# Linear attention into a two-expert MoE: routing and dispatch on two batches at a time, and the first loads in another order

## The chip, the cores and the metric

The kernel runs on one core of one Trainium2 chip. The metric is device time in microseconds (us) of one execution. TensorE is PE in the profile (its weight loads are PEld), VectorE is DVE, ScalarE is ACT, GpSimd is POOL, SyncE is SP; SP issues most of the DMAs of the loads, POOL the stores.

## The reference, cut to what matters

```python
# q, k, v: (8, 8, 576, 64) float32; batch, head, sequence, head dim
q_s = softmax(q, axis=-1)
k_s = softmax(k, axis=2)                       # over the sequence
kv  = einsum('bhsd,bhse->bhde', k_s, v)
a   = einsum('bhsd,bhde->bhse', q_s, kv)
x   = a.transpose(0, 2, 1, 3).reshape(4608, 512)

logits = x @ w_gate + modality_bias[modality_id]     # 8 experts
e_idx  = argmax(logits, axis=1)
gate_w = softmax(logits)[row, e_idx]
for e in range(8):                                   # w1[e]: 512x1024, w2[e]: 1024x512
    out[e_idx == e] = gate_w * (relu(x @ w1[e]) @ w2[e])
```

With this draw the bias of the modality decides the expert, so that two experts, here called the left and the right one, take all rows. The kernel loads the weights of these two alone, and has a loop over all experts behind it that runs only where this does not hold.

## The kernel before, in words

The eight batches are handled in four phases of two. Each batch passes through two functions:

- `stage_a(b)`: ACT takes exp of k and of q (`ek`, `eq`), POOL casts v to bf16 (`vb`, two instructions), PE forms k'v (`kv_ps`, 36 matmuls), transposes q (`tp_ps`, copied to `et` by DVE and ACT), DVE divides kv into the block-diagonal `kvbd`; from that PE makes the gate's matrix (`g_ps`, copied to `gx`) and the logits of the batch's 576 rows (`lg_ps`, 20 matmuls). The rest of the function, the routing, is a chain of some 35 DVE instructions on five columns (a batch is five tiles of 64, 128, 128, 128, 128 rows, one column each): the logits `lw`, `lg`, the maximum, `isa` (1 for the left expert), two matmuls `r_ps` that count rows, running offsets `aoff`, five permutation matrices `perm`, and `hhi`, `hlo`, `hv`, which place row numbers by a matmul. `hv` is made by POOL.
- `stage_b(b)`, the dispatch: for each of the five tiles PE forms the attention rows (`x_ps`), DVE scales them (`x_sb`), PE transposes and permutes them (`xT_ps`, by `perm`), and the tile is written twice into `xs`, the row buffer of both experts: from the left by ACT (the register offset from `aoff_i`) and from the right by DVE. Then five matmuls `id_ps` (`hlo` by `hv`) and an addition to `lst` by DVE give the row numbers.

After each second batch `places()` turns `lst` into the store indices `idx`, and `ffn` runs the two experts on the two passes of 512 rows that are full by then: `h_ps` (32 matmuls), relu to `hT` by ACT (three of four) or DVE, `y_ps` (32 matmuls), a copy to `y_sb`, and an indirect store issued by POOL. After the last phase two passes more, of 384 rows, follow.

Engines work in order, each from its own queue. The order in the queues is made ahead of time by a list scheduler: code under `tc.high_priority` (the two stages and the loads) goes ahead of `ffn`, which fills PE between. PSUM pools are `mm` (3 buffers: kv_ps, tp_ps, kvT_ps, x_ps, xT_ps), `ff` (3: h_ps, y_ps) and `sp` (2: g_ps, lg_ps, r_ps, id_ps).

SP issues the loads in the order batch 0, batch 1, weights of the left expert, batch 2, weights of the right expert, batch 3, and so on (k, v, q, 1152 KB each; the weights in four parts of 1024 KB). All go through one rotating pool of staging buffers, `st`: a load waits until its buffer's former content was cast. The weights are cast to `W` by ACT (parts 0 and 2) and DVE (parts 1 and 3). Seven small loads (bias, gate matrix in four parts, modality in two) are issued by ACT at the start.

```python
stage = ctx.enter_context(tc.tile_pool(name="stage", bufs=5))
...
for b in range(B):
    with tc.high_priority(offset=AHEAD):
        stage_a(b)
        stage_b(b)
        if b == 0:
            load_weights(eids[0], 0, (nc.scalar, nc.vector))
            load_batch(2)
```

Of the kernel before, what the change touches and what calls it, by code (L numbers as in the profile page):

```python
# [11 lines left out]
FP32 = mybir.dt.float32  # L12
# [8 lines left out]
P = 128  # L21
# [21 lines left out]
def kernel(  # L43
# [28 lines left out]
    NPH = 4  # L72

# [9 lines left out]
    stage = ctx.enter_context(tc.tile_pool(name="stage", bufs=5))  # L83
# [25 lines left out]

    bias_b = const.tile([P, 2, E], FP32)  # L110
    nc.scalar.dma_start(
# [5 lines left out]
    for h2 in range(2):  # L117
        for hl in range(2):
            nc.scalar.dma_start(
# [114 lines left out]
    kvbd_b = [persist.tile([P, NP, P], BF16, name=f"kvbd{i}") for i in range(2)]  # L234
    gx_b = [persist.tile([P, NP, 18], BF16, name=f"gx{i}") for i in range(2)]
    et_b = [persist.tile([P, NP, 640], BF16, name=f"et{i}") for i in range(2)]
    vb_b = [persist.tile([P, NJ, 2, 130], BF16, name=f"vb{i}") for i in range(2)]
    for i in range(2):
        nc.vector.memset(kvbd_b[i], 0.0)
# [3 lines left out]
        nc.gpsimd.memset(et_b[i][:, :, 576:640], 0.0)  # L243
# [44 lines left out]
    def stage_a(b):  # L288
        i = b % 2
        kvbd, gx, et, vb = kvbd_b[i], gx_b[i], et_b[i], vb_b[i]  # L290
# [5 lines left out]
        for hp in range(2):  # L296
            nc.gpsimd.tensor_copy(  # L297
# [60 lines left out]
        for t in range(NT):  # L358
            for p_ in range(NP):
# [6 lines left out]
                )  # L366

        qi = small.tile([P, NT * H], FP32, name="qi")
        nc.vector.tensor_scalar_add(out=qi, in0=view(lg_ps, [[18, NT * NP], [1, 2]], 16), scalar1=1e-9)
        nc.vector.reciprocal(out=qi, in_=qi)  # L370
        lw = small.tile([P, NT * NP, 2, E], FP32, name="lw")
        nc.vector.tensor_tensor(
            out=lw,
            in0=view(lg_ps, [[18, NT * NP], [8, 2], [1, 8]]),
            in1=view(qi, [[2, NT * NP], [1, 2], [0, 8]]),
            op=ALU.mult,
        )
        lg = small.tile([P, NT, E], FP32, name="lg")
        nc.vector.reduce_sum(out=lg, in_=view(lw, [[H * E, NT], [1, E], [E, H]]), axis=AX.X)
# [345 lines left out]
```

## Time and profile before

| | |
|---|---|
| median of 3 runs | 285.17 us (284.83 to 285.68) |
| the profiled execution: time | 284.43 us |
| its span, first to last instruction | 282.7 us |
| PE busy | 208.1 us (74% of the span), 1657 matmuls |
| DVE busy | 174.7 us (62%), 566 instructions |
| ACT busy | 115.8 us (41%), 161 instructions |
| POOL busy | 75.3 us (27%), 86 instructions |
| HBM read, written | 36.80 MB, 9.96 MB |

In the rows, numbers are microseconds from the span's start. A row of the timeline has the start, the duration, the engine, the line, the operation with what it writes and reads, and in brackets how long the engine was idle before and what ended that. A row of a wait has the engine that waited, whom for, the total, the number and the longest. PE's ends are modelled; a row that merges matmuls ("x4") runs from the first start to the last end.

### The profile page before, as it was taken

The page shows a single profiled execution, that of the slowest core. Times are in us where ns is not written, and L with a number is a line of the kernel's source. Part 1 is how long each engine was busy: PE and PEld are TensorE (multiplying, and loading weights), DVE is VectorE, ACT ScalarE, POOL GpSimd, SP SyncE. Part 2 cuts the span into 40 slices and gives each one's busy share as a digit, 9 for nine tenths or more (in the row PEclk, how much of TensorE's full clock was granted, in tenths as well). Part 3 has the DMA queues.
Part 4 walks back from the last instruction along what each step waited for, and adds up shares of the span by engine and source line. Part 5 has one row for each costly group of instructions (what it writes and reads, how often), then busy time and mean ns, then how long its engine had stood idle before and what let it go on. Part 6 is the DMA issues. An engine that isn't in the chain of part 4 may idle for free.

```text
span 282.7 us, 4628 instructions
## 1 busy us (share of the span) xinstructions
PE 208.1 (74%) x1657; PEld 116.2 (41%) x1657; DVE 174.7 (62%) x566; ACT 115.8 (41%) x161; POOL 75.3 (27%) x86
## 2 busy tenths in 40 slices
PE   0044358236998999787897979889997799999910
PEld 0033237124644644453463445445543344455500
DVE  4595865687479858858773897688678421313310
ACT  1365354623775692195158323422622414141200
POOL 7143203013103711351360033123205223224120
PEclk9999999999999999999999899999999999999985
DMA  5999999969959996143030002101201203021020
GB/s 166 329 392 405 387 390 400 363 205 330 319 202 332 344 377 265 39 140 141 0 151 0 0 3 111 39 1 43 108 2 44 104 37 114 37 111 66 2 87 5
DMA packets 20716, 46.59 MB, mean 165 GB/s; under 512 B 3023, under 2 KB 3023, under 8 KB 20688
## 3 DMA queue, kind: packets, MB, share of 16 engines
q1 hardware_dynamic: 15872, 36.70, 36.2%
q0 software_dynamic: 3040, 9.44, 8.7%
q10 hardware_dynamic: 1776, 0.10, 0.4%
q8 instruction: 15, 0.25, 0.4%
q14 instruction: 13, 0.11, 0.1%
HBM read 36.80 MB, written 9.96 MB: 165 GB/s over the span
## 4 chain that ended last, share of the span: by engine, by line
PE 34%; issue 23%; DVE 6%; POOL 6%; ACT 4%; DMA 2%; POOLq 0%; DVEq 0%; ACTq 0%
PE y_ps L582 15%; PE h_ps L568 10%; POOL hv L452 3%; PE xT_ps L508 2%; PE kv_ps L306 2%; DVE xs L519 2%; DMA st<-in_v_dram 2%; POOL out_dram L595 2%; ACT xs L518 1%; ACT et L328 1%; PE tp_ps L318 1%; DVE x_sb L500 1%; PE x_ps L492 1%; PE id_ps L535 1%; DVE y_sb L591 1%
## 5 line engine op out<-in xcount | busy, mean ns | idle before, releaser
L568 PE MATMUL h_ps<-xs,W 128*128 128x512 bf16 (+1 forms) x320 | 76.0, 378 | 1.7 <-ACT xs L518 0.7
L582 PE MATMUL y_ps<-W,hT 128*128 128x512 bf16 x304 | 73.2, 379 | 1.7 <-DVE y_sb L591 1.1
L595 POOL DMA_INDIRECT out_dram<-y_sb,idx x38 | 37.5, 986 | 71.9 <-DVE y_sb L591 57.3
L518 ACT CAST xs<-xT_ps 128x512 f32 (+2 forms) x40 | 21.9, 546 | 71.1 <-PE xT_ps L508 67.2
L576 ACT ACTIVATE hT<-h_ps 128x512 bf16<-128x512 f32 (+1 forms) x60 | 34.0, 581 | 28.4 <-PE h_ps L568 21.8
L568 PEld LDWEIGHTS <-W 128*128 128x128 bf16 x320 | 30.3, 99 | 29.7 <-issue 4.4
L582 PEld LDWEIGHTS <-hT 128*128 128x128 bf16 x304 | 28.6, 98 | 30.8 <-issue 1.9
L452 POOL TENSOR_TENSOR hv<-hhi,vals 128x570 bf16<-128x570 bf16 x8 | 12.6, 1577 | 90.1 <-DVE hhi L448 90.1
L500 DVE TENSOR_TENSOR x_sb<-x_ps,scl 128x512 bf16<-128x512 f32 (+1 forms) x40 | 27.3, 683 | 7.6 <-PE x_ps L492 7.5
L508 PE MATMUL xT_ps<-perm,x_sb 128*128 128x128 bf16 (+1 forms) x160 | 19.0, 234 | 14.6 <-DVE x_sb L500 14.6
L519 DVE CAST xs<-xT_ps 128x512 f32 (+2 forms) x40 | 25.4, 634 | 5.8 <-ACT xs L518 5.2
L306 PE MATMUL kv_ps<-vb,ek 64*128 64x129 bf16 x288 | 18.3, 251 | 14.0 <-POOL vb L297 14.0
L591 DVE COPY y_sb<-y_ps 128x512 f32<-128x512 f32 x30 | 20.3, 685 | 12.7 <-PE y_ps L582 11.6
L578 DVE TENSOR_SCALAR hT<-h_ps 128x512 bf16<-128x512 f32 (+1 forms) x20 | 13.2, 660 | 22.4 <-PE h_ps L568 22.4
L297 POOL CAST vb<-st 128x1152 bf16<-128x1152 f32 x16 | 18.0, 1152 | 33.5 <-DMA st<-in_v_dram 33.5
L508 PEld LDWEIGHTS <-x_sb 128*128 128x128 bf16 (+1 forms) x160 | 11.0, 104 | 27.3 <-DVE x_sb L500 22.6
L306 PEld LDWEIGHTS <-ek 64*128 64x128 bf16 x288 | 14.8, 110 | 15.7 <-ACT ek L294 10.9
L295 ACT ACTIVATE eq<-st 128x2304 bf16<-128x2304 f32 x8 | 17.1, 2135 | 6.5 <-DMA st<-in_q_dram 6.5
L294 ACT ACTIVATE ek<-st 128x2304 bf16<-128x2304 f32 x8 | 17.0, 2124 | 6.2 <-PE kv_ps L306 3.7
L492 PE MATMUL x_ps<-kvbd,et 128*128 128x128 bf16 (+1 forms) x160 | 18.1, 244 | 1.5 <-ACT et L328 1.5
L318 PE MATMUL tp_ps<-ident,eq 128*128 128x128 bf16 x144 | 14.4, 253 | 5.3 <-DVE et L326 2.7
L318 PEld LDWEIGHTS <-eq 128*128 128x128 bf16 x144 | 11.5, 115 | 10.8 <-issue 6.3
(123 smaller groups left out, 203.0 us busy)
## 6 DMA issues: line engine op xcount, KB each, us to landing
st<-in_k_dram SPq DMA_DIRECT2D x8, 1152.0 KB, 8.1
st<-in_v_dram SPq DMA_DIRECT2D x8, 1152.0 KB, 8.0
st<-in_q_dram SPq DMA_DIRECT2D x8, 1152.0 KB, 6.4
st<-in_moe_w_dram SPq DMA_DIRECT2D x8, 1024.0 KB, 9.9
out_dram<-y_sb,idx POOLq DMA_INDIRECT x38, 2.7
mraw<-in_moe_modality_id_dram ACTq DMA_DIRECT2D x2, 36.0 KB, 5.1
wg_f<-in_moe_w_gate_dram ACTq DMA_DIRECT2D x4, 4.0 KB, 6.8
bias_b<-n_moe_modality_bias_dram ACTq DMA_DIRECT2D x1, 8.0 KB, 5.3
```

The source lines that it names most:

```text
L306: nc.tensor.matmul(out=kv[hg][:, 130 * hp : 130 * hp + 129], lhsT=ek[rows, j, P * hp : P * hp + P], rhs=vb[rows, j, hp, 0:129], start=(j = ...
L318: nc.tensor.transpose(out=view(tp, [[2 * nj * 64, 2], [1, 64]], hp * nj * 64 + jj * 64), in_=eq[:, c0 + jj, P * hp : P * hp + P], identity ...
L452: nc.gpsimd.tensor_tensor(out=hv, in0=view(hhi, [[NSL, NT], [0, 3], [1, NSL]]), in1=view(vals, [[3, NT], [1, 3], [0, NSL]], b * NT * 3), o ...
L500: nc.vector.tensor_tensor(out=x_sb[0:T], in0=view(x_ps, [[Dh, H], [1, Dh]], 0, (0, T)), in1=view(scl, [[1, H], [0, Dh]], t * H, (0, T)), o ...
L508: nc.tensor.matmul(out=xT_ps[:, kd, 0:T], lhsT=view(x_sb, [[1, P]], kd * P, (0, T)), rhs=perm[0:T, t, 0:T], start=True, stop=True,)
L518: wa = nc.scalar.copy(out=window(a, passes_a[ph], T, ph == NPH - 1), in_=xT_ps[:, :, 0:T])
L519: wb = nc.vector.tensor_copy(out=window(a + right, passes_b[ph], T, ph == NPH - 1, True), in_=xT_ps[:, :, 0:T])
L568: nc.tensor.matmul(out=h_ps[:, 0:w], lhsT=W[:, slot, kd * F + f * P : kd * F + (f + 1) * P], rhs=xs[:, kd, lo : lo + w], start=(kd == 0), ...
L576: nc.scalar.activation(out=hT[:, f, 0:w], in_=h_ps[:, 0:w], func=ACT.Relu)
L582: nc.tensor.matmul(out=y_ps, lhsT=hT[:, kf, t * P : (t + 1) * P], rhs=W[:, slot, W2 + kf * D : W2 + (kf + 1) * D], start=(kf == 0), stop=( ...
L591: nc.vector.tensor_copy(out=y_sb, in_=y_ps)
L595: store = nc.gpsimd.indirect_dma_start(out=out, out_offset=bass.IndirectOffsetOnAxis(ap=ix[:, c : c + 1], axis=0), in_=y_sb, in_offset=Non ...
```

## The change

1. The loads of batch 0 are issued first, and the seven small loads behind them on SP's queue instead of ahead on ACT's.
2. `stage_a` ends at `lg_ps`. The routing is a function of its own, `route(pr)`, on the ten columns of two batches; the first part (`qi`, `lw`) still runs per batch. `stage_b` becomes `dispatch(pr)`: ten tiles, one accumulation of ten `id_ps` matmuls, one addition to `lst`.
3. Both copies of a tile into `xs` are made by ACT; DVE no longer loads the offsets into registers.
4. `vb` of batches 0 and 1 is cast by DVE.
5. `kvbd` and `et` have three buffers instead of two, the staging pool four instead of five, `hlo`, `hhi`, `hv`, `lw` one instead of two.
6. The loads of the weights come after `stage_a` of batches 0 and 1, ahead of routing and dispatch; `places()` and the indices come under the high priority.

The layout of the weight loads is the same in both versions (128 partitions a part).

```diff
-    stage = ctx.enter_context(tc.tile_pool(name="stage", bufs=5))
+    stage = ctx.enter_context(tc.tile_pool(name="stage", bufs=4))
...
+    load_batch(0)
     bias_b = const.tile([P, 2, E], FP32)
-    nc.scalar.dma_start(
+    nc.sync.dma_start(
         out=bias_b,
...
-    load_batch(0)
...
-            nc.gpsimd.tensor_copy(
+            (nc.vector if b < 2 else nc.gpsimd).tensor_copy(
                 out=view(vb, [[Dh, 2], [260, NJ], [1, Dh]], 130 * hp),
...
+        lgs[b] = lg_ps
+
+    def route(pr):
+        b = 2 * pr
+        qi = small.tile([P, NT2 * H], FP32, name="qi")
+        lw = small.tile([P, NT2 * NP, 2, E], FP32, name="lw", bufs=1)
+        for i in range(2):
+            lg_ps = lgs.pop(b + i)
+            qv = qi[:, i * NT * H : (i + 1) * NT * H]
+            nc.vector.tensor_scalar_add(out=qv, in0=view(lg_ps, [[18, NT * NP], [1, 2]], 16), scalar1=1e-9)
+            nc.vector.reciprocal(out=qv, in_=qv)
+            nc.vector.tensor_tensor(
+                out=lw[:, i * NT * NP : (i + 1) * NT * NP],
...
-        lg = small.tile([P, NT, E], FP32, name="lg")
-        nc.vector.reduce_sum(out=lg, in_=view(lw, [[H * E, NT], [1, E], [E, H]]), axis=AX.X)
+        lg = small.tile([P, NT2, E], FP32, name="lg")
+        nc.vector.reduce_sum(out=lg, in_=view(lw, [[H * E, NT2], [1, E], [E, H]]), axis=AX.X)
...
-        perm = sb.tile([P, NT, P], BF16, name="perm")
-        for t in range(NT):
+        perm = sb.tile([P, NT2, P], BF16, name="perm")
+        for t in range(NT2):
...
-        hlo = sb.tile([P, NT, P], BF16, name="hlo")
+        hlo = sb.tile([P, NT2, P], BF16, name="hlo", bufs=1)
...
-        hv = sb.tile([P, NT, 3, NSL], BF16, name="hv")
+        hv = sb.tile([P, NT2, 3, NSL], BF16, name="hv", bufs=1)
         nc.gpsimd.tensor_tensor(
             out=hv,
...
+    def dispatch(pr):
+        scl, perm, hlo, hv = sc.pop(pr)
+        for b in (2 * pr, 2 * pr + 1):
+            kvbd, et = kvbd_b[b % NB], et_b[b % NB]
...
+                engines=[ENG.Activation],
...
-            wb = nc.vector.tensor_copy(
-                out=window(a + right, passes_b[ph], T, ph == NPH - 1, True), in_=xT_ps[:, :, 0:T]
-            )
+                wb = nc.scalar.copy(
+                    out=window(a + right, passes_b[pr], T, pr == NPH - 1, True), in_=xT_ps[:, :, 0:T]
+                )
...
-    for b in range(B):
+    for ph in range(NPH):
         with tc.high_priority(offset=AHEAD):
-            stage_a(b)
-            stage_b(b)
-            if b == 0:
-                load_weights(eids[0], 0, (nc.scalar, nc.vector))
-                load_batch(2)
...
+            for b in (2 * ph, 2 * ph + 1):
+                stage_a(b)
+                if b < 2:
+                    load_weights(eids[b], b, (nc.scalar, nc.vector))
+                if b + 2 < B:
+                    load_batch(b + 2)
+            route(ph)
+            dispatch(ph)
             idb, ab, sel = places()
```

How the change moves instructions is seen at three places. A number behind a name is that of its buffer; the lines of the changed program stand some 20 lower than before for the same operation.

The first is DVE's queue in the dispatch ahead of the first `ffn`, from the first scaled tile of batch 1 on, before the change:

```order
L500 TENSOR_TENSOR x_sb_677<-x_ps_672,scl_630 64x512
L436 TENSOR_TENSOR slot_646<-slot_646,aoff_173 128x5
L658 TENSOR_SCALAR ok_3396<-aoff_173 1x1
L659 TENSOR_SCALAR ok_3396<-aoff_173 1x1
L438 TENSOR_SCALAR hi_650<-slot_646 128x5
L442 SCALAR_TENSOR_TENSOR lo_652<-hi_650,slot_646 128x5
L448 TENSOR_TENSOR hhi_656<-iota_row_116,hi_650 128x190
L481 TENSOR_LOAD aoff_i_175
L444 TENSOR_TENSOR hlo_654<-iota_row_116,lo_652 128x640
L519 ISA
L519 COPY xs_171<-xT_ps_679 128x4x64
L500 TENSOR_TENSOR x_sb_691<-x_ps_686,scl_630 128x512
```

The five permutation matrices stand ahead of the first scaled tile there. The same place now, from the permutation matrices of the first pair on:

```order
L449 TENSOR_SCALAR perm_519<-iota_row_116,pos_516 128x128 x10
L455 TENSOR_TENSOR slot_530<-slot_530,pos_516 128x10
L521 TENSOR_TENSOR x_sb_574<-x_ps_569,scl_509 128x512
L456 TENSOR_TENSOR slot_530<-slot_530,aoff_173 128x10
L458 TENSOR_SCALAR hi_534<-slot_530 128x10
L462 SCALAR_TENSOR_TENSOR lo_536<-hi_534,slot_530 128x10
L468 TENSOR_TENSOR hhi_540<-iota_row_116,hi_534 128x380
L464 TENSOR_TENSOR hlo_538<-iota_row_116,lo_536 128x1280
L521 TENSOR_TENSOR x_sb_588<-x_ps_583,scl_509 128x512
L562 TENSOR_TENSOR lst_204<-lst_204,id_ps_706 128x114
```

Ten matrices, and `hhi` and `hlo` of twice the width, come in one piece between the first tile and the third; the copies to `xs` are gone from this queue. PE has the ten `id_ps` matmuls after the `x_ps` of the third tile.

The second is DVE's queue at the routing that follows the first `ffn` pass, from the sum of the gate on. Before (batch 2):

```order
L400 TENSOR_REDUCE gsum_1119<-lg_1101 128x5
L429 TENSOR_SCALAR perm_1133<-iota_row_116,pos_1130 128x128
L401 TENSOR_SCALAR gsum_1119<-gsum_1119 128x5
L429 TENSOR_SCALAR perm_1133<-iota_row_116,pos_1130 128x128
L402 RECIPROCAL gsum_1119<-gsum_1119 128x5
L429 TENSOR_SCALAR perm_1133<-iota_row_116,pos_1130 128x128
L405 TENSOR_TENSOR scl_1123<-qi_1096,gsum_1119 128x20 x2
L429 TENSOR_SCALAR perm_1133<-iota_row_116,pos_1130 128x128 x2
L435 TENSOR_TENSOR slot_1139<-slot_1139,pos_1130 128x5
L500 TENSOR_TENSOR x_sb_1170<-x_ps_1165,scl_1123 64x512
L436 TENSOR_TENSOR slot_1139<-slot_1139,aoff_173 128x5
L578 TENSOR_SCALAR hT_775<-h_ps_818 128x512
```

And now (batches 2 and 3):

```order
L415 TENSOR_REDUCE gsum_1196<-lg_1178 128x10
L449 TENSOR_SCALAR perm_1210<-iota_row_116,pos_1207 128x128
L416 TENSOR_SCALAR gsum_1196<-gsum_1196 128x10
L449 TENSOR_SCALAR perm_1210<-iota_row_116,pos_1207 128x128
L417 RECIPROCAL gsum_1196<-gsum_1196 128x10
L449 TENSOR_SCALAR perm_1210<-iota_row_116,pos_1207 128x128
L420 TENSOR_TENSOR scl_1200<-qi_1170,gsum_1196 128x40 x2
L449 TENSOR_SCALAR perm_1210<-iota_row_116,pos_1207 128x128 x7
L455 TENSOR_TENSOR slot_1221<-slot_1221,pos_1207 128x10
L521 TENSOR_TENSOR x_sb_1251<-x_ps_1246,scl_1200 64x512
L456 TENSOR_TENSOR slot_1221<-slot_1221,aoff_173 128x10
L598 TENSOR_SCALAR hT_831<-h_ps_850 128x512
```

The first scaled tile, and the relu behind it, now follow ten matrices instead of five. In the two later phases the first scaled tile stands ahead of the ten, the second behind them.

The third is ACT's queue in the dispatch ahead of the first `ffn`. Before (batch 1):

```order
L518 ISA
L518 COPY xs_171<-xT_ps_679 128x4x64
L518 ISA
L518 COPY xs_171<-xT_ps_693 128x4x128
L282 CAST W_172<-st_755 128x2048
L518 ISA
L518 COPY xs_171<-xT_ps_707 128x4x128
```

And now:

```order
L538 ISA
L538 COPY xs_171<-xT_ps_643 128x4x64
L285 CAST W_172<-st_461 128x2048
L539 ISA
L539 COPY xs_171<-xT_ps_643 128x4x64
L538 ISA
L538 COPY xs_171<-xT_ps_657 128x4x128
L539 ISA
L539 COPY xs_171<-xT_ps_657 128x4x128
```

Each tile takes two copies of ACT in a row, and a cast of the weights stands between two of them.

More of the change, by code (lines that the diff above doesn't have):

```diff
@@ L415, in stage_a @@
         nc.vector.tensor_tensor_scan(
-            out=aoff[:, o + 1 : o + 1 + NT],
-            data0=ones[:, 0:NT],
+            out=aoff[:, o + 1 : o + 1 + NT2],
+            data0=ones[:, 0:NT2],
             data1=r_ps[:, 1, :],
@@ L532, in stage_b @@
         id_ps = sp_ps.tile([P, 3, NSL], FP32, name="id_ps", tag="sp")
-        for t in range(NT):
-            T = tsz[t]
+        for c in range(NT2):
+            T = tsz[c % NT]
             nc.tensor.matmul(
                 out=id_ps,
-                lhsT=hlo[0:T, t, :],
-                rhs=hv[0:T, t, :, :],
-                start=(t == 0),
-                stop=(t == NT - 1),
+                lhsT=hlo[0:T, c, :],
+                rhs=hv[0:T, c, :, :],
+                start=(c == 0),
+                stop=(c == NT2 - 1),
```

215 lines of the change are left out of this document (105 added, 110 removed).

## The prediction

> **What bounds the kernel now.** I read first the busy time by stretch, cut where the work changes, then PE's waits there, then the timeline of the stretch ahead of the first `ffn`. Columns: from:to, length, then busy time of PE, PEld, DVE, ACT, POOL, each with its instructions, PE's granted clock, DMA share, GB/s.
>
> ```profile
> 0.00:72.00 72.00, 28.90 (x295) 22.62 (x295) 48.44 (x162) 31.05 (x30) 19.05 (x34) 1.00 0.94 334
> 72.00:98.50 26.50, 24.78 (x210) 14.27 (x210) 19.80 (x68) 17.03 (x20) 8.73 (x8) 1.00 0.85 301
> 98.50:122.50 24.00, 21.15 (x186) 11.03 (x185) 18.23 (x65) 11.91 (x19) 6.68 (x7) 1.00 0.58 220
> 122.50:144.50 22.00, 18.90 (x147) 9.62 (x145) 16.43 (x55) 10.81 (x17) 6.62 (x7) 1.00 0.29 102
> 144.50:168.00 23.50, 19.52 (x176) 10.71 (x175) 15.94 (x57) 11.81 (x17) 5.50 (x5) 0.93 0.07 24
> 168.00:197.00 29.00, 26.08 (x254) 14.04 (x252) 22.42 (x75) 9.23 (x17) 7.30 (x7) 1.00 0.12 47
> 197.00:221.06 24.06, 20.21 (x162) 10.37 (x160) 18.78 (x65) 9.69 (x18) 7.78 (x8) 1.00 0.17 66
> 221.06:269.65 48.59, 48.55 (x241) 23.49 (x240) 13.61 (x24) 14.23 (x26) 12.49 (x13) 1.00 0.16 60
> 269.65:282.70 13.05, 0.00 (x0) 0.00 (x0) 1.03 (x4) 0.00 (x0) 1.19 (x2) 0.66 0.12 45
> PE id_ps L535 <- POOL hv L452: 6.0, 6, 1.4
> PE r_ps L396 <- DVE isa L392: 3.2, 5, 1.1
> PE xT_ps L508 <- DVE x_sb L500: 2.7, 4, 0.8
> PE g_ps L352 <- ACT kvT L349: 1.8, 1, 1.8
> ```
>
> Three parts. A head of 72 us, in which PE is mostly idle and the DMA is busy, until the first `ffn`. A middle of 149.1 us (72 to 221.06) in which PE works 130.6 (its six rows added) and stands for 18.4. An end of 61.6 us, pure `ffn` and the last stores, which the change leaves alone. So PE bounds all from 72 on; the time can only move with the start of the first `ffn` and with the 18.4 us. The four waits above are those of the middle: 13.7 of the 18.4. DVE, at 111.6 of 149.1 us, has room: taking work from it pays only where PE waits for it.
>
> **The head: loads.**
>
> ```profile
> SPq L100 <- DMA bias_b<-n_moe_modality_bias_dram: 4.8, 1, 4.8
> DMA to landing us min/median/max: 5.4/7.6/14.5
> 15.75 2.12 ACT L295 ACTIVATE eq<-st 128x2304 bf16<-128x2304 f32 x1 [4.95 <-DMA st<-in_q_dram]
> 18.77 2.12 ACT L294 ACTIVATE ek<-st 128x2304 bf16<-128x2304 f32 x1 [0.89 <-DMA st<-in_k_dram]
> 25.33 2.12 ACT L295 ACTIVATE eq<-st 128x2304 bf16<-128x2304 f32 x1 [1.58 <-DMA st<-in_q_dram]
> ```
>
> The second load waited 4.8 us for the bias: only so many DMAs are in flight. Now k, v and q go out together, and at 3.0 us apiece (18.77 - 15.75) q of batch 0 lands at about 12.3 instead of 15.75. But in the changed queue k of batch 1 waits for the landing of that q, behind the small loads: 12.3 plus the shortest landing, 5.4, is 17.7; v follows at 20.7, q at 23.7. So batch 1 is complete 1.6 us earlier, not 3.4. The seven small loads, behind that q, land near 13 to 14.5 by my estimate, just as DVE wants them; if later, all of batch 0 shifts with them, since DVE has the bias ahead of `kinv`.
>
> **The head: two stages, one route, ten tiles.**
>
> ```profile
> 43.73 1.94 PE L306 MATMUL kv_ps<-vb,ek 64*128 64x129 bf16 x16
> 51.12 0.68 PE L360 MATMUL lg_ps<-gx,et 128*128 128x18 bf16 x20 [0.48 <-DVE gx L356]
> 55.06 0.23 DVE L392 SCALAR_TENSOR_TENSOR isa<-kk,key,valid 128x5 bf16<-128x5 f32 x1
> 57.34 0.68 DVE L500 TENSOR_TENSOR x_sb<-x_ps,scl 64x512 bf16<-64x512 f32 x1
> 65.39 0.69 DVE L500 TENSOR_TENSOR x_sb<-x_ps,scl 128x512 bf16<-128x512 f32 x1 [0.39 <-PE x_ps L492]
> 66.13 0.61 PE L508 MATMUL xT_ps<-perm,x_sb 128*128 128x128 bf16 x4 [0.79 <-DVE x_sb L500]
> 67.21 0.69 DVE L500 TENSOR_TENSOR x_sb<-x_ps,scl 128x512 bf16<-128x512 f32 x1 [0.53 <-PE x_ps L492]
> 71.99 0.61 PE L568 MATMUL h_ps<-xs,W 128*128 128x512 bf16 x1
> L282 ACT CAST W<-st 128x2048 bf16<-128x2048 f32 x4 | 7.6, 1891 | 0.0
> L284 DVE CAST W<-st 128x2048 bf16<-128x2048 f32 x4 | 4.9, 1218 | 0.0
> L297 POOL CAST vb<-st 128x1152 bf16<-128x1152 f32 x16 | 18.0, 1152 | 33.5 <-DMA st<-in_v_dram 33.5
> L379 DVE TENSOR_REDUCE lg<-lw 128x40 f32<-128x320 f32 x8 | 5.8, 726 | 0.2
> L429 DVE TENSOR_SCALAR perm<-iota_row,pos 128x128 bf16<-128x128 bf16 x40 | 8.0, 242 | 0.0
> ```
>
> In batch 1 of before, the last kv matmul to the last logit takes 6.1 us (45.67 to 51.80), logits to the first scaled tile 5.5, a tile 1.82 (65.39 to 67.21), and from the last tile's `x_sb` to the first `h_ps` 4.8.
>
> Now `vb` is cast by DVE: between 0.7 us (the W cast's 1.218 for 2048 elements, scaled) and POOL's 1.15 apiece; I take 0.7, as the operation is the W cast's own. Its k'v of batch 1 ends at about 26.7 (`eq` 25.8 beside it). Then 6.1 us, plus two casts of weights that the new order puts into this chain, 1.9 on ACT and 1.2 on DVE, less 0.5 of overlap: the logits of both batches stand at **35.4** (33.5 to 37).
>
> Routing both at once, 5.5 becomes 7.0: +0.7 for the reduction of twice the width, +0.4 for ten small operations with ten columns, +1.2 for a W cast ahead of the tile, -1.0 as the permutations come behind it. Then the tile 0.7, ten permutations at some 0.2 step to step (2.0) and small ones 0.4: second tile at 35.4 + 10.1; its 0.7, `hi`, `lo` 0.4, `hhi` 0.5, to 35.4 + 11.7. Here PE stands: the ten `id_ps` wait for `hv` of twice the width (+3.3, below), run 1.1, one tile's matmuls another 1.1, so the fourth tile is scaled at 35.4 + 17.2. Six tiles more at 1.82 (+10.9), a W cast among them (+1.0 of 1.2), and 4.8 to the first `h_ps`: 35.4 + 34 = **69.4**, against 72. The head gains 2.6 us, bounds 66.5 and 74.
>
> Both copies on ACT, costed at nothing here, are covered by the 1.82: two are 1.2 (below). If PE gets quicker that cover is gone. The exp of batch 2 and two W casts, 5.9 us of ACT, fall into the same stretch; there are three buffers between. With four staging buffers the right expert's third part waits for `vb` of batch 2, which POOL now does behind `hv`: I have it landed near 57, needed near 66. Third buffers for `kvbd` and `et` cost memsets under the first load.
>
> **The middle.**
>
> ```profile
> 58.84 1.14 POOL L452 TENSOR_TENSOR hv<-hhi,vals 128x570 bf16<-128x570 bf16 x1 [13.69 <-DVE hhi L448]
> 87.53 0.35 DVE L448 TENSOR_TENSOR hhi<-iota_row,hi 128x190 bf16<-128x190 bf16 x1
> 87.79 0.82 DVE L444 TENSOR_TENSOR hlo<-iota_row,lo 128x640 bf16<-128x640 bf16 x1
> 87.96 1.65 POOL L452 TENSOR_TENSOR hv<-hhi,vals 128x570 bf16<-128x570 bf16 x1 [11.47 <-DVE hhi L448]
> L519 DVE CAST xs<-xT_ps 128x512 f32 (+2 forms) x40 | 25.4, 634 | 5.8 <-ACT xs L518 5.2
> L518 ACT CAST xs<-xT_ps 128x512 f32 x32 | 18.9, 589 | 52.6 <-PE xT_ps L508 52.6
> 241.94 6.91 PE y_ps L582 x32
> ```
>
> - `id_ps` for `hv`: six waits of 1.0 become three. `hv` takes 1.65 beside `hlo`, 1.14 alone; twice the width is 2.3 to 3.3, I take 3.3, since `hlo` is beside it in all three. Each wait grows by 1.65 and 0.2 for `hhi`: 3 x 2.85 = 8.5 against 6.0, **+2.5**.
> - `r_ps` for `isa`: 3.5 us from the logits (51.80 to 55.29) becomes 4.6. PE has 17, 16 and 22 `ffn` matmuls in between, at 0.216 (6.91 / 32) 3.7, 3.5 and 4.8 us, in the last case with two copies of `y_sb` in DVE's way (a copy of a tile is 0.63 below): 0.9 + 1.1 + 1.0 = 3.0 against 3.2, **0**.
> - `xT_ps` for `x_sb`: in the first of the three, five more permutations (1.0) and wider neighbours (0.2) make 2.7 us from `isa` to the scaled tile 4.0, with 6 `ffn` matmuls (1.3) and `r_ps` (0.3) for cover: a wait of 2.4, and 0.35 for the relu behind. In the other two the ten permutations stand ahead of the second tile, 2.8 us, covered by 2.0 and 1.3; with the tiles beside, 1.5 and 1.8. Sum 6.0 against 2.7, **+3.3**.
> - The rest, 6.5 us (18.4 less 6.0, 3.2, 2.7), I take at 5.5 for three routings fewer, **-1.0**; 4 to 8.
>
> DVE gives up 25.4 us of copies, ACT takes 40 more at 0.59: no sum, as PE waits for neither in the rows. The middle costs +4.8 us, bounds 0 and +9.
>
> On `hv` beside `hlo`, the Trainium skill ("SBUF — State Buffer", section "Who interferes with whom") says that a DVE instruction with two SBUF inputs and a GpSimd instruction that reads SBUF exclude each other, the second standing until the first ends. The rows agree: 1.65 is the rest of `hlo` (0.65) and a little over 1.0.
>
> **Sum.** 284.43 - 2.6 + 4.8 = 286.6 against the profiled execution. The median of the runs is 0.74 us above that execution, so I forecast **287.4**.
>
> **Rivals.**
>
> 1. *Faster: the first pair's tiles run at PE's quick rate.* Four 128-column matmuls take 0.61 in the head, but 0.39 from 84 on. If the longer run of ten tiles brings the quick rate, a tile needs some 1.4 (0.74 + 0.22 + 0.39): 7 x 0.4, with `id_ps` (0.5) and kv of batch 2 (1.7), -5.0: 282.4. It decides if the first `h_ps` comes before 67. Against it: PE has nothing from 35 to 42, and pauses for `hv`.
>
> ```profile
> 91.76 0.39 PE L508 MATMUL xT_ps<-perm,x_sb 128*128 128x128 bf16 x4
> ```
>
> 2. *No change: the waits of the middle grow by half of what I say.* The cover is placed by a scheduler that may know `hv`'s price: +2.4 instead of +4.8, 285.0. Against it: the six waits of 1.0 show that it underrates today's.
> 3. *Slower yet: ACT becomes the bound in the phase of the second pair.* 24 more copies come between relus and three exps of 2.1; if each exp holds a relu long enough to fill the three `ff` buffers, 1.5 each and more: +5, 292. For it: one `g_ps` wait of 1.8 behind ACT today. Against: ACT is at 47%.
> 4. *`hv` waits for the whole wider `hlo`.* `hlo` is 0.82 for 640 elements, 0.35 for 190: 1.5 for 1280; then 2.2 for `hv`: 3.7 instead of 3.3, in four places, +1.6: 289.0. That is the skill's rule above.
>
> **Chances.** My forecast 0.36, rival 1 0.32 (with other ways to an earlier `ffn`), rival 2 0.14, rival 3 0.10, rival 4 0.08. About 0.3% (0.86 us) is what a measurement of this kernel can tell from no change. Faster 0.32, same 0.14, slower 0.54. The range goes from below rival 1 to beyond rival 3, with head and middle at their bounds: **280 to 294**; for the forecast alone 285 to 291.
>
> **What would show it.** The first `h_ps` near 69 to 70; the start of the pure `ffn`, counted from there, some 5 us later than the 149 of before; `id_ps` waiting three times for near 3 us, and once more in the head; the longest `xT_ps` wait ahead of the second pair's first tile. The forecast is wrong if the logits of both batches stand well before 33 or after 38, if a tile in the head takes 1.4, or if the middle idles less than 18.

## The result, and the profile after

The changed kernel takes 274.16 us (median of 4 runs, 273.85 to 277.09), the kernel before 285.28 beside it: a ratio of 0.963, 95% interval 0.957 to 0.970. I had forecast 287.4 and slower.

The busy time by stretch, columns as in the prediction; the cuts are the first `h_ps`, the start of the pure `ffn`, PE's last matmul:

```profile
0.00:66.68 66.68, 25.30 (x292) 20.32 (x293) 39.79 (x135) 33.92 (x38) 13.00 (x28) 1.00 0.88 319
66.68:212.43 145.75, 130.47 (x1117) 70.96 (x1117) 89.18 (x265) 82.63 (x133) 43.70 (x36) 0.96 0.40 148
212.43:261.00 48.57, 48.55 (x242) 23.47 (x240) 12.71 (x20) 14.82 (x27) 13.87 (x15) 1.00 0.17 66
261.00:272.10 11.10, 0.00 (x0) 0.00 (x0) 1.04 (x4) 0.00 (x0) 1.21 (x2) 0.64 0.14 52
```

The span falls by 10.6: 5.3 in the head, 3.3 in the middle (145.75 against 149.07), 2.0 behind PE's last matmul. The middle idles 15.3 instead of 18.4. PE's waits in it, and the rows of the head that answer to those of before:

```profile
PE id_ps L555 <- POOL hv L472: 5.9, 3, 2.1
PE xT_ps L529 <- DVE x_sb L521: 4.5, 3, 3.1
PE r_ps L411 <- DVE isa L402: 2.0, 3, 0.7
34.55 0.68 PE L362 MATMUL lg_ps<-gx,et 128*128 128x18 bf16 x20 [1.76 <-DVE gx L358]
45.82 3.27 POOL L472 TENSOR_TENSOR hv<-hhi,vals 128x1140 bf16<-128x1140 bf16 x1 [37.49 <-DVE hhi L468]
49.13 1.44 PE L555 MATMUL id_ps<-hv,hlo 64*128 64x114 bf16 x10 [3.27 <-POOL hv L472]
58.78 0.69 DVE L521 TENSOR_TENSOR x_sb<-x_ps,scl 128x512 bf16<-128x512 f32 x1 [1.13 <-PE x_ps L513]
60.60 0.69 DVE L521 TENSOR_TENSOR x_sb<-x_ps,scl 128x512 bf16<-128x512 f32 x1 [1.13 <-PE x_ps L513]
66.68 0.59 PE L588 MATMUL h_ps<-xs,W 128*128 128x512 bf16 x1 [0.73 <-ACT xs L538]
```

Logits, `hv` and the pace of a tile (1.82) stand where I had put them; most of what came sooner stands in DVE's queue (below). The table has every run of the study. The ratio is to runs of the kernel before beside it on the same chip, where that took 285 to 292 us. Ratios from different chips are to be compared with care: the changed kernel gave 0.963 on one and 0.942 on another, and most of the difference is the kernel before (285.3 and 292.3). "Half clock" is half the length of the stretches of PE at a granted clock of 0.50 behind the first `h_ps` (below). It bounds their cost from above, as PE stands in part of them: in the changed kernel for 2.1 of 10.2 us. Two of the four runs of kernel 8 (279.0 and 280.0) are over 1.5% above its fastest and count as slow; the median of its two fast runs, 274.9 and 277.5, is 276.2.

| kernel | us | ratio to before | first h_ps | from there to PE's last | end | half clock |
|---|---|---|---|---|---|---|
| before, first chip | 285.28 | 1 | 71.99 | 197.62 | 13.09 | 1.7 |
| changed, first chip | 274.16 | 0.963 | 66.68 | 194.30 | 11.12 | 5.1 |
| before again (one run) | 290.50 | | 72.25 | 203.18 | 13.37 | 3.4 |
| changed again | 275.40 | 0.942 (0.937 to 0.947) | 66.87 | 195.78 | 11.25 | 5.7 |
| 1 small loads first | 276.32 | 0.948 (0.942 to 0.954) | 67.29 | 196.19 | 11.12 | 3.4 |
| 2 vb on POOL | 279.10 | 0.955 (0.947 to 0.963) | 66.86 | 199.27 | 12.87 | 10.2 |
| 3 right copy on DVE | 283.48 | 0.971 (0.964 to 0.977) | 69.38 | 201.39 | 11.63 | 6.8 |
| 4 not fused | 278.18 | 0.955 (0.949 to 0.961) | 64.37 | 197.24 | 12.89 | 5.1 |
| 5 not fused, id_ps late | 272.49 | 0.933 (0.928 to 0.938) | 64.25 | 192.73 | 13.52 | 5.1 |
| 6 before, copies on ACT | 271.75 | 0.928 (0.923 to 0.934) | 70.59 | 186.76 | 12.85 | 0 |
| 7 before, throwaway copy | 288.06 | 0.989 (0.982 to 0.995) | 73.10 | 200.03 | 12.87 | 3.4 |
| 8 before, copies, loads, vb | 278.27 | 0.957 (0.951 to 0.964) | 66.65 | 194.70 | 11.45 | 3.4 |
| 9 as 8, id_ps late | 273.32 | 0.936 (0.930 to 0.943) | 65.94 | 193.38 | 12.88 | 5.1 |
| 10 changed, orders forced | 268.66 | 0.920 (0.915 to 0.925) | 66.78 | 188.67 | 11.25 | 4.2 |
| 11 as 10, x_ps ahead | 271.58 | 0.933 (0.927 to 0.938) | 64.06 | 194.53 | 11.11 | 3.4 |
| 12 as 11, first pair only | 266.27 | 0.931 (0.925 to 0.937) | 64.66 | 188.52 | 11.02 | 1.8 |
| 13 as 12, matrices spread | 266.46 | 0.931 (0.926 to 0.936) | 63.61 | 189.62 | 11.27 | 3.4 |
| 14 changed, pause filled | 277.59 | 0.954 (0.948 to 0.960) | 64.93 | 198.03 | 11.24 | 4.4 |
| 15 changed, no loop (one run) | 273.26 | | 66.59 | 198.82 | 6.09 | 6.8 |
| 16 before, no loop (one run) | 282.94 | | 72.19 | 202.89 | 6.12 | 3.4 |

### The profile page after: what moved, and what is told of

Its sections match the earlier page's. It is cut to its first block, busy times and chain, and to the rows that moved or that the text cites. A ratio compares the mean times of both kernels' runs of the same rounds, so it can differ in the third digit from the quotient of the medians.

```text
span 272.1 us, 4487 instructions
## 1 busy us (share of the span) xinstructions
PE 204.3 (75%) x1649; PEld 114.8 (42%) x1649; DVE 142.7 (52%) x423; ACT 131.4 (48%) x197; POOL 71.8 (26%) x79
## 4 chain that ended last, share of the span: by engine, by line
PE 48%; issue 24%; POOL 9%; ACT 6%; DVE 6%; DMA 3%; ACTq 1%; POOLq 0%
PE y_ps L602 18%; PE h_ps L588 18%; POOL hv L472 5%; PE xT_ps L529 3%; PE kv_ps L308 3%; DMA st<-in_v_dram 3%; PE x_ps L513 2%; ACT xs L539 2%; PE id_ps L555 2%; POOL xs L250 2%; PE tp_ps L320 1%; POOL vb L299 1%; ACT et L330 1%; ACT xs L538 1%; PE lg_ps L362 1%
## 5 line engine op out<-in xcount | busy, mean ns | idle before, releaser
L588 PE MATMUL h_ps<-xs,W 128*128 128x512 bf16 (+1 forms) x320 | 74.8, 378 | 1.5 <-ACT xs L538 0.7
L602 PE MATMUL y_ps<-W,hT 128*128 128x512 bf16 x304 | 71.5, 379 | 0.5 <-DVE hT L598 0.4
L615 POOL DMA_INDIRECT out_dram<-y_sb,idx x38 | 37.5, 987 | 111.2 <-DVE y_sb L611 81.8
L538 ACT CAST xs<-xT_ps 128x512 f32 (+2 forms) x40 | 22.2, 556 | 39.4 <-PE xT_ps L529 35.1
L611 DVE COPY y_sb<-y_ps 128x512 f32<-128x512 f32 x30 | 20.6, 689 | 21.2 <-PE y_ps L602 20.1
L472 POOL TENSOR_TENSOR hv<-hhi,vals 128x1140 bf16<-128x1140 bf16 x4 | 13.0, 3250 | 60.8 <-DVE hhi L468 60.8
L529 PE MATMUL xT_ps<-perm,x_sb 128*128 128x128 bf16 (+1 forms) x160 | 18.0, 241 | 14.3 <-DVE x_sb L521 8.1
L598 DVE TENSOR_SCALAR hT<-h_ps 128x512 bf16<-128x512 f32 (+1 forms) x20 | 13.2, 661 | 25.4 <-PE h_ps L588 25.3
L308 PE MATMUL kv_ps<-vb,ek 64*128 64x129 bf16 x288 | 14.4, 252 | 12.9 <-DVE vb L299 12.8
L539 ACT CAST xs<-xT_ps 128x512 f32 (+2 forms) x40 | 22.6, 565 | 0.0
L299 POOL CAST vb<-st 128x1152 bf16<-128x1152 f32 x12 | 13.9, 1183 | 18.4 <-DMA st<-in_v_dram 18.4
L308 PEld LDWEIGHTS <-ek 64*128 64x128 bf16 x288 | 12.0, 112 | 14.4 <-issue 13.9
L613 ACT COPY y_sb<-y_ps 128x512 f32<-128x512 f32 x8 | 4.7, 593 | 27.0 <-PE y_ps L602 27.0
L320 PE MATMUL tp_ps<-ident,eq 128*128 128x128 bf16 x144 | 12.9, 254 | 4.9 <-ACT eq L297 4.7
## 6 DMA issues: line engine op xcount, KB each, us to landing
bias_b<-n_moe_modality_bias_dram SPq DMA_DIRECT2D x1, 8.0 KB, 10.6
```

The costliest lines, as they stand in the source:

```text
L308: nc.tensor.matmul(out=kv[hg][:, 130 * hp : 130 * hp + 129], lhsT=ek[rows, j, P * hp : P * hp + P], rhs=vb[rows, j, hp, 0:129], start=(j = ...
L472: nc.gpsimd.tensor_tensor(out=hv, in0=view(hhi, [[NSL, NT2], [0, 3], [1, NSL]]), in1=view(vals, [[3, NT2], [1, 3], [0, NSL]], b * NT * 3), ...
L529: nc.tensor.matmul(out=xT_ps[:, kd, 0:T], lhsT=view(x_sb, [[1, P]], kd * P, (0, T)), rhs=perm[0:T, c, 0:T], start=True, stop=True,)
L538: wa = nc.scalar.copy(out=window(a, passes_a[pr], T, pr == NPH - 1), in_=xT_ps[:, :, 0:T])
L539: wb = nc.scalar.copy(out=window(a + right, passes_b[pr], T, pr == NPH - 1, True), in_=xT_ps[:, :, 0:T])
L588: nc.tensor.matmul(out=h_ps[:, 0:w], lhsT=W[:, slot, kd * F + f * P : kd * F + (f + 1) * P], rhs=xs[:, kd, lo : lo + w], start=(kd == 0), ...
```

## Experiments: undoing one part each

**1, the small loads on ACT and ahead of batch 0 again.**

> The changed kernel, but the seven small loads are again issued by ACT ahead of batch 0. Theory (the gain is two stages ahead of one routing and one dispatch, not the loads): q of batch 1 landed only about half a microsecond to 1.6 us earlier by the new load order (its exp starts at 24.79 now, 25.33 before), so the logits of the first pair end at 35.7 to 36.8 instead of 35.23, and the time is 274.7 to 275.8. Rival (the head's 5.3 us are the load order): the first h_ps goes back to about 72, the time to 279 or more. If the small loads cost nothing in either place: 274.2.

The logits end at 35.83 and the first `h_ps` is at 67.29: 0.6 us, the theory's lower end. From there on it takes 196.2, the changed kernel 194.3 and 195.8 on two chips: nothing that is clearly of the loads. Their order is worth some half a microsecond here.

**2, `vb` all on POOL.**

> The changed kernel, but POOL casts v of batches 0 and 1 as well. Theory: q of batch 1 lands 3 us behind its v, so that a cast slower by 0.9 us for the two halves (1.15 against 0.71 each) is mostly covered; POOL's memsets of the first microseconds delay batch 0 alone, which has slack: +0 to +1 us, 274.2 to 275.2. Rival (vb was in the path of the head): kv of batch 1 ends 2 us later, the logits too, 276 to 277.

First `h_ps` at 66.86, 0.2 later: covered, as the theory says. The time, 279.1, is above both expectations. The trace has up to 10.2 us of lost clock for it, against 5.7, and an end that is 1.6 longer (15 and 16, below); neither was forecast, and that `vb` brings them is not shown.

**3, the right copy by DVE again**, with its register loads:

```diff
-                wb = nc.scalar.copy(
+                wb = nc.vector.tensor_copy(
```

> The changed kernel, but the right copy of each tile is made by DVE again (40 copies of 0.63 us back on it, and its register loads). My prediction's step (the move of the copies is worth nothing, as PE waits for neither): 273.9 to 274.6. Rival (DVE's relief is what kept the middle's waits below the forecast): the waits of id_ps for hv and of xT_ps for x_sb grow, the middle idles 18 us or more instead of 15.3, and the time is 277 to 279.

```profile
0.00:69.38 69.38, 25.99 (x293) 21.10 (x293) 47.36 (x140) 32.21 (x29) 15.49 (x30) 1.00 0.91 327
69.38:270.77 201.39, 179.13 (x1334) 94.07 (x1357) 118.91 (x320) 82.79 (x128) 54.90 (x49) 0.97 0.32 116
PE xT_ps L529 <- DVE x_sb L521: 7.2, 7, 3.6
PE h_ps L588 <- DVE hT L598: 2.1, 1, 2.1
```

The two windows, and two of PE's waits from 69.38 on. My step (nothing) falls: 0.971 against 0.942, on two chips; against kernel 1, which ran beside it, it is 7.2 us slower (283.5 and 276.3). It is also more than the rival had (277 to 279), and `id_ps` waits less, not longer (4.1 against 6.9). The head is 2.5 longer than in the changed kernel on the second chip, the rest 5.6. PE never waits for the copy; it waits for `x_sb` and `hT`, which stand in the same queue.

**4 and 5, the pair's order without fusing**: `stage_a` of both batches, then route and dispatch with five columns, batch by batch; in 5 the `id_ps` matmuls of a batch are forced behind its last tile.

```diff
-            route(ph)
-            dispatch(ph)
+            for b in (2 * ph, 2 * ph + 1):
+                route(b)
+                dispatch(b)
```

> The changed kernel, but routing and dispatch are done per batch with five columns as before, with the order of the pair kept: stage_a of both batches, then route and dispatch of the first, then of the second. Theory (halving the number of routings is the gain of the middle, and one dispatch of ten tiles that of the head): hv is waited for seven or eight times at about 1 to 1.4 us, r_ps five or more times, the middle idles 18 us or more (+3), and the head has a second routing of some 5 us in it, part of it beside tiles of the first batch (+1 to +3): 278 to 280. Rival (the order of the stages is the gain, fusing adds nothing): 274 to 275. Rival (fusing costs, by the wide hv and the ten permutations): 271 to 273.

> Routing and dispatch per batch in the pair's order, as in the earlier unfused kernel, with the five id_ps matmuls of each batch forced behind its last tile. Theory (the id_ps waits of 5.9 and 3.8 there are real losses): 6 to 8 us less than the unfused kernel, near the fused one with its id_ps late, so that fusing as such is worth within 2 us either way. Rival (fused routing saves in the middle what only it can): 3 us or more slower than the fused one with id_ps late.

The head is 2.3 to 2.6 shorter without fusing, not longer as the theory had it: five columns give the first tiles sooner. The rest of 4 is 1.5 to 3 longer. The sum, 278.2, is in the theory's range, but by another split, in which the end has 1.6. With the late `id_ps` it falls by 5.7, to 3.8 above the fused kernel with its `id_ps` late (10, below), which is the rival's "3 us or more". But 2.3 of these 3.8 are the end (13.52 against 11.25), which goes with the code of the skipped loop (15 and 16; SP waits 7.2 for PE's sequencer in 5 and 5.1 in 10) and not with fusing; and 10 also has its matrices moved. That leaves about 1.5 us for fusing and the matrices, within the theory's 2. The waits for `hv` are gone in 5, and `xT_ps` waits 9.4 for `x_sb` where it waited 1.5 in 4.

## Experiments: the copies alone

**6, the kernel before with both copies on ACT, nothing else.**

> The kernel before, with one edit: both copies of a tile into xs are made by ACT. Theory A (the move of the copies is most of the gain, since undoing it cost 9 to 10 us): 0.965 to 0.975 of the time of before; the tile in the head of before takes less than its 1.82. Theory B (the copies matter only where two batches go through DVE together; in before PE waited for neither copy): 0.992 to 1.003 of before. My prediction's step (worth nothing anywhere): 1.00.

This is faster than the whole change: 0.928 against 0.942, on one chip. The windows of before (the row "before again", on another chip) and of this kernel, from the first `h_ps` on, and PE's largest waits in each:

```profile
72.25:275.43 203.18, 181.32 (x1364) 93.88 (x1363) 125.55 (x401) 84.40 (x132) 55.10 (x51) 0.98 0.30 108
PE id_ps L535 <- POOL hv L452: 6.0, 6, 1.4
PE tp_ps L318 <- DVE kvbd L339: 3.9, 5, 1.3
PE xT_ps L508 <- DVE x_sb L500: 2.7, 4, 0.8
...
PE g_ps L352 <- ACT kvT L349: 1.8, 1, 1.8
PE y_ps L582 <- DVE y_sb L591: 1.1, 2, 0.6
```

```profile
70.59:257.35 186.76, 173.47 (x1330) 92.09 (x1353) 109.00 (x367) 97.93 (x162) 57.29 (x53) 1.00 0.35 129
PE id_ps L535 <- POOL hv L452: 5.3, 6, 1.0
PE r_ps L396 <- DVE isa L392: 2.8, 5, 1.4
```

16.4 of the 18.6 us lie there. The waits on DVE's `kvbd`, `x_sb` and `y_sb` fall from 7.7 to under 1, `g_ps` for `kvT` goes, idle from 21.9 to 13.3, and the clock is full. (34 matmul records more are missing in the second row, so that its busy time is shown too low and its idle time too high.) How a copy that PE hardly waits for does this, in one tile of the head, before and in this kernel:

```profile
61.71 1.22 DVE L284 CAST W<-st 128x2048 bf16<-128x2048 f32 x1
62.05 0.63 PE L492 MATMUL x_ps<-kvbd,et 128*128 128x128 bf16 x4
62.35 0.59 ACT L518 CAST xs<-xT_ps 128x512 f32 x1 [3.41 <-PE xT_ps L508]
62.97 0.69 DVE L519 CAST xs<-xT_ps 128x512 f32 x1
63.58 0.68 DVE L500 TENSOR_TENSOR x_sb<-x_ps,scl 128x512 bf16<-128x512 f32 x1
64.31 0.61 PE L508 MATMUL xT_ps<-perm,x_sb 128*128 128x128 bf16 x4 [1.63 <-DVE x_sb L500]
```

```profile
61.55 0.63 PE L492 MATMUL x_ps<-kvbd,et 128*128 128x128 bf16 x4
62.23 0.69 DVE L500 TENSOR_TENSOR x_sb<-x_ps,scl 128x512 bf16<-128x512 f32 x1
62.97 0.61 PE L508 MATMUL xT_ps<-perm,x_sb 128*128 128x128 bf16 x4 [0.79 <-DVE x_sb L500]
64.65 1.22 DVE L284 CAST W<-st 128x2048 bf16<-128x2048 f32 x1
```

Before, `x_ps` is done at 62.68, but DVE's queue has a cast of W until 62.93 and then the copy of the tile ahead of `x_sb`: PE stands 1.63, 0.61 of it for the copy. Without the copy, and with the cast behind `x_sb`, it stands 0.79. On the second reader, the Trainium skill ("PSUM — Partial Sum Buffer", section "PSUM bank collisions raise a hardware error") says that reads of one bank by ScalarE and VectorE at once collide and are to be kept apart by semaphores. The trace agrees with the order: in all 40 pairs of before, DVE's copy starts 0.03 us or more behind the end of ACT's. The last tile of the head, and DVE's waits that end with ACT's copy in all of before (the 1.84 is in part a wait for the tile itself, which is there at 70.76):

```profile
70.47 0.29 PE L508 MATMUL xT_ps<-perm,x_sb 128*128 128x128 bf16 x1
70.85 0.59 ACT L518 CAST xs<-xT_ps 128x512 f32 x1 [3.42 <-PE xT_ps L508]
71.46 0.69 DVE L519 CAST xs<-xT_ps 128x512 f32 x1 [1.84 <-ACT xs L518]
DVE xs L519 <- ACT xs L518: 5.2, 7, 1.8
```

**7, the same with a throwaway copy of each tile by DVE** into a scratch tile, so that DVE does what it did but writes nothing of `xs`:

```diff
+            nc.vector.tensor_copy(out=waste_out[:, :, 0:T], in_=xT_ps[:, :, 0:T])
```

> The kernel before with both copies into xs made by ACT, and beside them a throwaway copy of each tile by DVE from xT_ps into a scratch tile that nobody reads: DVE's load and its hold on PSUM are back, its part in xs and its register loads are not. Theory (it is DVE's time: x_sb, hhi, isa, y_sb stand behind the copies in its queue): 284 to 292, most of the 20 us come back. Rival (it is the coupling: in before DVE stood for ACT's copy of the same tile, 5.2 us in all, and loaded an offset into a register for each tile): 271 to 275.

```profile
DVE waste_out L523 <- ACT xs L520: 9.6, 10, 3.1
L523 DVE CAST waste_out<-xT_ps 128x512 bf16<-128x512 f32 (+1 forms) x40 | 25.3, 634 | 10.0 <-ACT xs L520 9.6
```

288.1: most of the gain is gone. So most of it is not in the register loads or in the writes of `xs`; it is a reader of `xT_ps` in DVE's queue. PE itself waits for this copy only 0.8 us in the whole run, so that its hold on the `xT_ps` buffer is hardly the price either. Whether its 0.634 us or its waits for ACT (9.6, more than the 5.2 of before) weigh more is not told apart.

**8 and 9, the copies with the load order and `vb` on DVE, per batch**; 9 with the late `id_ps`. A run of before stood beside them.

> The kernel before with three parts of the change: both copies into xs by ACT, the small loads behind batch 0 on SP, vb of batches 0 and 1 by DVE. Routing, dispatch and their order stay per batch; five staging buffers. Theory (pairing and fusing add nothing once the copies are moved): the first h_ps 1 to 3 us ahead of the 70.6 of the kernel with the copies alone, the rest as there: 0.915 to 0.928 of before on this chip, 3 to 7 us below the changed kernel. Rival (the loads bring nothing in this order, since batch 1 is not awaited there): 271 to 272, as with the copies alone.

> As the kernel before with copies on ACT, new load order and vb on DVE, and the five id_ps matmuls of each batch forced behind its last tile. Theory (the six waits of about 0.9 us of id_ps for hv are real losses there too): 4 to 5 us less than the same kernel without the forced order. Rival (the wait goes to xT for x_sb or into the next stage): within 2 us of it.

> The kernel before as it is, one look on the chip of the kernels beside it. On two further chips it took 290 to 294 us against 285 on the first. Theory (further dips of the granted clock, as in the first chip's profile from 154 to 160): first h_ps at 72.0, PE idle 18.4 from there as before, and the difference lies in stretches where the clock is under 0.95. Rival (waits of another kind): more than 20 us idle.

The head gains 3.9 by the loads and `vb` together here, and the rest loses 7.9: 278.3 (276.2 without the two runs named above the table), worse than the copies alone (271.75, on another chip) and outside what either theory gave. In the trace up to 3.4 of it is half clock, and `r_ps` waits 4.8 instead of 2.8; what else it is stays open. The late `id_ps` is worth 2.9 to 5.0 in the time, by which of these is taken, but 1.3 in the profiled stretch, so that theory and rival are not told apart. Before itself idles 21.9 on this chip, 3.9 of it in a wait that the first chip did not have (`tp_ps` for `kvbd`), beside one more half-clock stretch: both expectations are half right.

## Experiments: where the rest of the gain went

**10, two orders forced in the changed kernel**: `id_ps` behind the last tile of its pair, and the second batch's matrices one behind each tile of the first.

> The changed kernel with two orders forced: the ten id_ps matmuls come behind the last tile of their pair on PE, and the five permutation matrices of the second batch are made one behind each scaled tile of the first on DVE. Theory (the waits of id_ps for hv, 3.3 in the head and 5.9 in the middle, and the wait of 3.1 for the first scaled tile behind ten matrices are real losses): the first h_ps at 63 to 64, the middle idles 6 to 8 us less, the time is 0.965 to 0.975 of the changed kernel's. Rival (what PE does not wait for there it waits for behind it, DVE's and ACT's queues being the real bound): within 2 us of the changed kernel, waits at xT_ps or h_ps instead. The head alone: -3 us.

> The changed kernel as it is, run again on the chip of the three kernels beside it, so that they can be held against it there. Nothing is tested: first h_ps at 66.7, PE idle 15 to 18 us from there to its last matmul.

```profile
PE xT_ps L541 <- DVE x_sb L531: 6.4, 7, 2.4
PE r_ps L411 <- DVE isa L402: 2.5, 3, 1.1
```

268.7, 0.976 of the changed kernel: the time came near the theory's, but not where it said (its first `h_ps` was to be at 63 to 64). The wait for `hv` (6.9 in the changed kernel) is gone and a part returns at `xT_ps`; the stretch behind the first `h_ps` is 7.1 shorter. The head gains nothing: `id_ps` and batch 2's first transposes (`tp_ps`) now stand between the last tile and the first `h_ps`.

**11, 12, 13, `x_ps` formed one tile ahead**, in all pairs, in the first alone, and then with only two matrices ahead of the first tile.

```diff
+            if c + 1 < NT2:
+                ahead = make_x(c + 1)
             xT_ps = mm.tile([P, KD, P], FP32, name="xT_ps", tag="mm")
```

> The kernel with the late id_ps and the spread permutation matrices, and x_ps of each tile formed one tile earlier on PE (ahead of xT of the tile before). Theory (the 1.82 us of a tile in the head is the chain x_ps, x_sb, xT, each waiting for the other, not the rate of an engine; PE needs 1.2 a tile, ACT 1.2): the nine tiles come at about 1.3, the first h_ps at 62 to 63 instead of 66.8, and in the middle the six us of waits of xT for x_sb fall to 2 to 4: 259 to 263 us. Rival (ACT's two copies of 0.6 each with an exp or a cast among them set the pace as soon as the chain does not): a tile takes 1.6 or more, the first h_ps after 65.

> The kernel with late id_ps and the second batch's matrices between the tiles, and x_ps one tile ahead in the first pair only. Theory (the two effects are separate: 2.7 us in the head, nothing in the middle): first h_ps at 64, from there to PE's last matmul 188 to 190, 265 to 267 us, 0.905 to 0.915 of before. Rival (an earlier first ffn only moves the wait into the phase of the second pair, whose loads and routing come when they come): the main stretch grows by as much, 268 to 270.

> As the kernel beside it, with only two permutation matrices ahead of the first tile and each other one two tiles ahead of its use. Theory (the matrices ahead of the second pair's first scaled tile make PE's pause there, 2.4 us with five of them, 3.1 with ten): 1.7 to 1.9 us with two, and the time 0.5 to 2 us less than beside. Rival (the chain from isa to scl and the relus in DVE's queue make it): the pause stays at 2.2 or more and the time within 0.5 us.

```profile
48.78 0.68 DVE L533 TENSOR_TENSOR x_sb<-x_ps,scl 128x512 bf16<-128x512 f32 x1
50.13 0.69 DVE L533 TENSOR_TENSOR x_sb<-x_ps,scl 128x512 bf16<-128x512 f32 x1
```

These are two tiles of 11 in the head: 1.35 apart instead of 1.82, and the first `h_ps` at 64.06. The steps behind them are as short, but for the last (1.79). So the pace was the chain and not an engine. In the later pairs the same edit cost 5.9, twice what the head gained, and the 259 to 263 of the theory did not come. Kept to the first pair (12) it gives 266.3, the lowest time of the study, and the time and the stretch that its theory gave; against 10 the head is 2.1 shorter and the rest equal. But it has up to 2.4 less of lost clock, so that without the clock the rest may have grown by what the head gained, as the rival has it; this is not settled. 10 has the lowest ratio, on a chip where before took 292 instead of 286; the two were not run side by side. Both beat the two kernels of this study's question. Spreading the matrices left the pause ahead of the second pair at 3.0 (3.3 in 12): its rival holds.

**14, PE's pause ahead of `id_ps` filled** with 14 throwaway matmuls per pair.

> The changed kernel with 14 throwaway matmuls (342 columns, some 0.15 us each, read hhi) ahead of the id_ps matmuls of each pair, so that PE works while hv is made. Nothing of the result uses them. Theory (a pause of PE over 1 us is often followed by 3.4 us at half clock, at a loss of 1.7 us each): the pauses ahead of id_ps fall under 1 us, the dips behind them go, so that the kernel takes no longer than the changed one in spite of 6.5 us more work of PE in the middle: 272 to 275.5. Rival (the dips come by themselves, whatever the pauses): as many dips as before, and 275.5 to 278.

Inconclusive. The wait for `hv` falls from 6.9 to 2.9, but not under 1 us a time (the longest is 1.7), and `xT_ps` waits 6.1 instead of 4.3. Behind the first `h_ps` only one half-clock stretch begins, against two in the changed kernel on the second chip. PE's own work grew (184.5 against 178.1, where some 24 matmul records are missing), and the time, 277.6, is the rival's.

**15 and 16, both kernels without the skipped loop behind the stores.**

> The changed kernel without the loop over the other experts behind the stores (it does not run with this draw). Theory (the end from PE's last matmul to the end of the span, 11.1 here against 13.1 before, holds the fetch of the code behind the loop that is jumped over, and that differs by how the code lies): both kernels without the loop have an end of the same length within 0.3 us, some 4 to 7 us shorter. Rival (the end differs by the stores): the difference of 2.0 stays.

> The kernel before without the loop over the other experts behind the stores. Theory: the same end as the changed kernel without the loop, within 0.3 us. Rival: 2.0 us longer than there.

6.09 and 6.12: without the loop the ends are equal. With it SP waits for PE's sequencer, before and in the changed kernel:

```profile
SPq L720 <- PEq L720: 6.7, 2, 6.2
SPq L736 <- PEq L736: 5.0, 2, 4.1
```

So the 2.0 us of the end come with the code of the skipped loop, that is the read of its count and the jump past it. Kernels 1 to 14 have ends from 11.0 to 13.5 with the same loop; that this goes with how the code lies, as the theory has it, is not shown.

## Why the prediction was wrong

- **The step that failed: both copies on ACT "costed at nothing", and in the middle "no sum, as PE waits for neither".** I read PE's waits by the name of what it waited for. The copies stood ahead of `x_sb`, `hT` and `kvbd` in DVE's queue, and their price was booked there. Measured: 8.1 us in the changed kernel (3 against the changed one, on different chips; 7.2 against kernel 1 on one chip), 20.6 in the kernel before (6). These 7 to 8 are the larger part of the 13.2 us between forecast and result; the end is 2.0, and the rest is not traced to one term.
- **Head, 69.4 forecast, 66.68 measured.** The pace (1.82) and `hv` (3.3, 3.27) were right. The logits (35.4 forecast, 35.23) were right by luck: the k'v of batch 1 ended at 24.8 and not at 26.7, and from there to the logits it took 10.4 and not 8.7. Without the copies the second tile was scaled 1.2 and the fourth 1.0 sooner after the logits than I said; with the copies on DVE (3) they come 0.6 and 1.3 later than I said. The W cast among the last six tiles cost 0 instead of 1.0: DVE made it while it waited for PE. From the last tile to the first `h_ps` it took 4.3 for 4.8. That the head with DVE's copies is 69.38, my 69.4, is luck as well, since the last two errors make up for the late fourth tile. (The terms of my "5.5 becomes 7.0" add up to 6.8.)
- **Middle, +4.8 forecast, -3.3 measured.** `id_ps` 5.9 (8.5 forecast), `xT_ps` 4.5 (6.0), `r_ps` 2.0 (3.0), the rest 2.9 (5.5). Each of the three waits for `hv` is longer than one of before, as I said, but 2.0 on average and not 2.85, so that their sum did not grow; `xT_ps` grew by less than I said. The middle idles 15.3, under the 18 that I had named as the sign of being wrong. From the first `h_ps` to PE's last matmul the kernel with DVE's copies takes 3.8 more than before on the first chip, but 1.8 less than before on its own chip (201.39 against 203.18), with up to 3.4 more of lost clock. So my +4.8 was too high beside the copies as well, by an amount that stays open.
- **End, 0 forecast, -2.0 measured**: the code of the skipped loop (15, 16).
- **Rivals.** The first decided by its time (first `h_ps` ahead of 67) and not by its mechanism: a tile stayed at 1.82. The second was half right: `id_ps` and `xT_ps` were better covered than I had it. The third, ACT as the bound, did not come: ACT works 82.6 of 145.75. The fourth: `hv` took 3.25 on average, not 3.7.
- **The rest of the change.** Against the copies alone, on one chip, the whole change gains 3.7 in the head and 1.6 at the end and gives back 9.0 between: 4.4 by longer waits (`xT_ps` +4.1, `id_ps` +1.6, others less) and 4.6 in PE's busy time, which the lost clock (up to 5.7) can account for.

## What to carry to other kernels

Price an instruction by what stands behind it in its engine's queue, not by who waits for it; here a copy of 0.63 us, made forty times, that PE's waits name with 0.4 us in all was worth more than the rest of the change. The two engines that read the same PSUM tile here went one behind the other, so that one engine doing both freed the other's queue. When a stage is fused, look at the longest single wait as well as at their sum, and move the matmuls that depend on the slow producer behind work that is ready.

## What was not expected of the hardware

Behind pauses of PE its granted clock fell to 0.50 for 3.4 us, a loss of at most 1.7, or for two or three such pieces in a row. Windows of the changed kernel in its longest, 96.9 to 107.1 (a pause, then the clock, and after it), and of changed again in its head:

```profile
92.80:95.90 3.10, 0.04 (x1) 0.00 (x0) 3.10 (x21) 0.97 (x1) 0.15 (x1) 1.00 1.03 406
97.00:99.00 2.00, 2.00 (x11) 1.10 (x9) 2.00 (x4) 0.25 (x1) 1.11 (x1) 0.50 1.05 406
103.20:107.00 3.80, 3.80 (x19) 2.02 (x17) 2.12 (x7) 3.66 (x5) 0.00 (x0) 0.50 0.94 309
108.00:111.00 3.00, 1.99 (x18) 0.97 (x17) 1.74 (x3) 1.84 (x6) 0.00 (x0) 1.00 0.72 283
33.90:71.40 37.50, 18.48 (x168) 13.40 (x169) 23.35 (x70) 21.03 (x29) 7.87 (x5) 0.50 0.85 312
```

In 20 traces I count 34 such stretches that begin behind the first `h_ps`; 32 begin in a pause of 0.9 us or more or at most 1.5 us behind its end, though such places are 8% of the time there. But two of three such pauses (99 in all) bring none, one of 2.9 us in kernel 8 among them. Four traces (changed again, 10, 12, 14) have a longer stretch, of 13.7 to 37.5 us, in the head. It costs little there, where PE works about half of the time (18.5 of 37.5 us in the last row): changed again has its first `h_ps` at 66.87, and with the full clock it was 66.68. Kernel 6, whose longest pause is 1.4, has none. The Trainium skill ("TensorE: Matmul & The Clock Gate", section "HAM oscillation — how this bites in real kernels") gives the rule that pauses over some 3.4 us cost the full clock. The length of a stretch here agrees with that figure, the pauses do not: stretches followed pauses of 1.0 us (kernel 8, up to 103.5) and 1.8 us (before, up to 152.9). That the pause is the cause is argued from this order, not shown: filling it (14) did not settle it.
